# Order of the first slot's turn, group 5's gate, the first weight splits and the first biases in the head of a convolution with routed feed-forward

## Chip, cores, metric

One core of a Trainium2 chip runs the kernel. The time is device microseconds (us) of one execution, lower is better. Engines are named as in the profile: PE is TensorE (PEld its weight loads), DVE is VectorE, ACT is ScalarE, POOL is GpSimd, SP is SyncE, which here only issues DMAs. A letter q behind an engine's name is its instruction queue.

## What is computed

```python
# x (8, 3584, 192); weight (8 heads, 7 taps); modality_id (28672,); w_gate (192, 8); modality_bias (2, 8); w1 (8, 192, 1024); w2 (8, 1024, 192)
w = softmax(weight, axis=-1)                                  # 7 taps for each head of 24 channels
x = einsum('hk,bskhg->bshg', w, windows(x)).reshape(28672, 192)   # causal convolution along s
logits = x @ w_gate + modality_bias[modality_id]
e_idx, gate_w = argmax(logits), softmax(logits)[e_idx]
for e in range(8):                                            # one expert for each row
    mask = e_idx == e
    out[mask] = gate_w[mask, None] * (relu(x[mask] @ w1[e]) @ w2[e])
```

All is fp32. Products of fp32 data are taken in parts of TensorE's fast fp32 format: a value is split into a rounded part (a cast on ACT, "hi") and the rest (a subtraction on DVE, "lo").

## The kernel before

The rows of x come in 19 groups, of 1, 1, 2, 2, 2 and then 4 quads; a quad is 4 tiles of 112 rows. Groups 0 to 4 are chunk 0, groups 5 and 6 chunk 1, and so on. `body` takes a group through: eight convolutions, one for each head (`cv`, L282), copied from PSUM into the group's `y` buffers by ACT or DVE (L287, L289); the bias of its rows (`bias_of`, tile `bt`, two POOL instructions, L296 and L299); then for each quad a transposition on DVE (`turned`, L306), for groups from 5 on a split of it (`gx`, L98 cast on ACT and L99 subtraction on DVE), the product with the gate (`gt`, L326), its transposition (`lt`, L333) and the sum with the bias (`lg`, L336, L338); and the choice of an expert (`choose`, L349 to L366). `place` follows while the next group is convolved: counts by two products (`rp`, L376, L377), a scan (L382), positions (`pos`, L388, L389), their reduction (`row`, L391) and the row numbers (`idx`, L393). Then `send` scatters the group's rows from `y` to DRAM (`routed_rows`, L210, an indirect DMA on POOL for each tile). There are four `y` buffers: groups 0 to 4 hold y0, y1, y2, y3, y0, group 5 holds y1 and y2, group 6 y3 and y0. A buffer is free for the next group's convolutions when its scatters have landed.

A slot is up to 1024 rows of one expert. Its weights come by DMA (`raw1`, `raw2`) and are split (`w1b`, 4 parts, and `w2b`, 4 parts, by L98 and L99). Its rows come back from DRAM (`rows`, `ends`, `tags`, L661) after the last scatter of its chunk, are transposed on DVE (`turn`: `tp`, L688 and L689) and split into `sxh`, `sxl` and `sxs` (L696, L698). A step multiplies 128 hidden units (`hps`, five products, L712, two PSUM banks), applies relu on ACT (`hh`, L715), takes the rest on DVE (`hl`, L716), and two steps later multiplies by the second weights (`po`, L730, L734).

The head ends in `start(0)` (L903): all of chunk 0's groups, the first slot's loads, four splits of its first weights, then 26 steps (`AHEAD`) of the following groups' work, of which the gate's last instruction up to step 18 (`PIN`) is kept, and then the slot's `turn(0)`, to be placed behind that instruction. From there `run` emits steps of slots and pieces of groups side by side. A scheduler that simulates the engines places the emitted instructions in each engine's queue; each queue runs in order. In `run`, ACT keeps the order of emission. The convolutions of groups from 5 on, their gate products and their `rp` share two PSUM banks in turn (`bank`, tag t): group 5's gate halves take one each, group 6's head 0 and head 1 follow, then `rp`, then head 2 on head 1's bank, which so waits for head 1's copies.

Of the kernel before, what the change touches and what calls it, by code (L numbers as in the profile page):

```python
# [18 lines left out]
P = 128  # L19
# [7 lines left out]
WARM2 = 0  # L27
WAIT = 3
OUTS = 4
PIN = 18  # L30
AHEAD = 26
UNIT = 256
LONG = 512
# [10 lines left out]
def conv_then_routed_ffn(ctx, tc, x, weight, modality, w_gate, mod_bias, w1, w2, out):  # L44
# [89 lines left out]
    def make_bands():  # L134

        wide = P + MB
        line = raw1[0][0:1].rearrange("p c n -> p (c n)")[:, 0:H * wide].rearrange("p (h u) -> p h u", h=H)
        nc.vector.memset(line, 0.0)
        taps = const.tile([1, H, K], F32, name="taps")
        nc.sync.dma_start(out=taps, in_=weight.unsqueeze(0))  # L140
        peak = const.tile([1, H], F32, name="peak")
        nc.vector.tensor_reduce(out=peak, in_=taps, axis=AX.X, op=ALU.max)
        nc.vector.tensor_tensor(out=taps, in0=taps, in1=peak.unsqueeze(2).broadcast_to([1, H, K]), op=ALU.subtract)
        nc.scalar.activation(out=taps, in_=taps, func=AF.Exp)
        tot = const.tile([1, H], F32, name="tot")
        nc.vector.tensor_reduce(out=tot, in_=taps, axis=AX.X, op=ALU.add)
        nc.vector.tensor_scalar(out=tot, in0=tot, scalar1=1e-9, scalar2=None, op0=ALU.add)
        nc.vector.reciprocal(out=tot, in_=tot)

        first = MB - 1 + HALO - K + 1  # L150
        nc.vector.tensor_tensor(out=line[:, :, first:first + K], in0=taps,
                                in1=tot.unsqueeze(2).broadcast_to([1, H, K]), op=ALU.mult)
        lines = nc.dram_tensor("tap_lines", (H, wide), F32, kind="Internal").ap()
        nc.sync.dma_start(out=lines.unsqueeze(0), in_=line)
        band = xp.tile([P, H, MB], F32, name="band", tag="xr_0")
        nc.sync.dma_start(out=band, in_=bass.AP(lines.tensor, 0, [[1, P], [wide, H], [1, MB]]))
        hi = const.tile([P, H, MB], F32R, name="band_hi")
        lo = const.tile([P, H, MB], F32R, name="band_lo")
        split(hi, lo, band)
        return band, hi, lo  # L160

    def make_gate():


        wg = const.tile([P, NK, E], F32, name="wg")
        for q in range(P // Q):
            nc.scalar.dma_start(out=wg[q * Q:(q + 1) * Q], in_=w_gate.rearrange("(k c) e -> c k e", c=Q))
        wgs = const.tile([P, NK, 2 * E], F32R, name="wgs")
        nc.scalar.copy(out=wgs[:, :, 0:E], in_=wg)
        nc.vector.tensor_tensor(out=wgs[:, :, E:2 * E], in0=wg, in1=f(wgs[:, :, 0:E]), op=ALU.subtract)  # L170
        whole = const.tile([P, NK, P], F32, name="wg_whole", tag="w2b1")
# [58 lines left out]
    class Group:  # L230
# [60 lines left out]
        def bias_of(self):  # L291
            n = self.blocks
            self.lg = rt.tile([MB, NT, E], F32, name="lg")[:, 0:self.tiles]
            self.bt = rt.tile([MB, NT, E], F32, name="bt", bufs=1)[:, 0:self.tiles]
            m = mt[:, self.b0:self.b0 + self.nb, self.block:self.block + n].rearrange("p b s -> p s b")
            nc.gpsimd.tensor_tensor(  # L296
                out=self.bt.rearrange("p (s b) e -> p s b e", s=n), in0=m.unsqueeze(3).broadcast_to([MB, n, self.nb, E]),
                in1=step.unsqueeze(1).unsqueeze(1).broadcast_to([MB, n, self.nb, E]), op=ALU.mult)
            nc.gpsimd.tensor_tensor(out=self.bt, in0=self.bt,  # L299
                                    in1=start_row.unsqueeze(1).broadcast_to([MB, self.tiles, E]), op=ALU.add)  # L300
# [8 lines left out]
        def part_turned(self, q):  # L309
# [4 lines left out]
                both = xp.tile([P, 2, NK, NB, Q], F32R, name="gx", tag=self.place_x)  # L314
                self.gh, self.gl = both[:, 0, :, 0:self.nb], both[:, 1, :, 0:self.nb]
            at = slice(4 * q % NB, 4 * q % NB + 4)
            split(self.gh[:, :, at], self.gl[:, :, at], self.turned)
            return [(wg_parts, self.gh), (wg_parts, self.gl)]

        def gate(self, terms):  # L320
# [293 lines left out]
    class Slot:  # L614
# [59 lines left out]
        def split(self, part):  # L674

            i = self.i % 2
            if part < 4:
                c, ns = part % 2, slice(part // 2 * FF // 2, (part // 2 + 1) * FF // 2)
                split(w1b[i][:, c, ns], w1b[i][:, 2 + c, ns], raw1[i][:, c, ns])
            else:  # L680
                cs = slice((part - 4) * NF // 4, (part - 3) * NF // 4)
                split(w2b[i][:, cs, 0:D], w2b[i][:, cs, D:2 * D], raw2[i][:, cs, :])
# [220 lines left out]
    def start(i):  # L903
# [1 line left out]
            through("groups", 0)  # L905
            w2b.append(const.tile([P, NF, 2 * D], F32R, name="w2b1"))
        bring(lots.index((i, 0)))
        for part in range(4 if i == 0 else 8):
            made[i].split(part)
        for n in range(AHEAD if i == 0 else 0):  # L910
            advance()
            if n < PIN:
                pin = state["gate"]
        with tc.issue_after(pin) if i == 0 else nullcontext():
            warm(WARM2 if i == 0 else 0)
            made[i].turn(0)
# [35 lines left out]
```

## Time and profile before

| What | us |
|---|---|
| Three timed runs, median | 1293.76 (1290.85 to 1293.97) |
| Profiled execution | 1280.46, its span 1278.7 |
| PE busy | 1225.4 of the span |
| DVE busy | 975.8 |
| ACT busy | 692.6 |
| POOL busy | 543.5 |

The profiled execution is read as a time line that starts at 0. Behind the first 200 us PE has hardly a gap; the head, in which the first groups are convolved and scattered and the first slot is made ready, has most of PE's idle time. A row of the time line gives start, duration, engine, line, operation, output and input, count, and in brackets the idle time of that engine just before and what ended it.

### The profile page before, as it was taken

To read this page: it belongs to the slowest core of one execution; us is meant where nothing else is said; L and a number is where in the kernel's file an instruction comes from. 1 tells how busy PE (TensorE), PEld (TensorE's weight loads), DVE (VectorE), ACT (ScalarE), POOL (GpSimd) and SP (SyncE) were. 2 spreads that over 40 slices of the span, in tenths; PEclk is the share of its full clock that TensorE was granted. 3 is DMA by queue.
4 is the path that set the end of the run, shared out by engine and by line. 5 is a ranking of instruction groups with operands and counts; after the bars stand their busy time and mean duration, and the time that the engine had idled before them with its cause. 6 is when DMAs were issued, how large, how long until landed. Compare 5 with 4: busy or idle time off the path is not lost.

```text
span 1278.7 us, 23361 instructions
## 1 busy us (share of the span) xinstructions
PE 1225.4 (96%) x6986; PEld 1091.8 (85%) x6986; DVE 975.8 (76%) x2280; ACT 692.6 (54%) x1485; POOL 543.5 (43%) x574
## 2 busy tenths in 40 slices
PE   9568899999999999999999999999999999999996
PEld 7347778888898989898898889899898888888996
DVE  5668877787888778877888778877776666577895
ACT  2235565555555555555565656556545445446784
POOL 4736645344545343444545344353546221122222
PEclk9869999999999999999999999999999999999999
DMA  6578554426462445324363535344424244395341
GB/s 174 159 193 183 150 128 94 121 50 150 91 162 53 108 96 132 105 58 111 68 149 98 135 80 146 75 92 101 96 46 127 54 83 101 81 249 123 93 90 33
DMA packets 311420, 141.89 MB, mean 111 GB/s; under 512 B 225650, under 2 KB 297963, under 8 KB 311284
## 3 DMA queue, kind: packets, MB, share of 16 engines
q1 hardware_dynamic: 285668, 94.95, 35.5%
q0 software_dynamic: 23232, 44.30, 10.9%
q8 instruction: 57, 0.93, 0.3%
q10 hardware_dynamic: 2384, 1.06, 0.3%
q14 instruction: 79, 0.65, 0.2%
HBM read 118.16 MB, written 51.82 MB: 133 GB/s over the span
## 4 chain that ended last, share of the span: by engine, by line
PE 72%; DVE 9%; issue 7%; ACT 3%; POOL 2%; DMA 2%; DVEq 0%; SPq 0%; POOLq 0%; ACTq 0%
PE hps L712 34%; PE po L730 21%; PE po L734 10%; PE cv L282 5%; PE gt L326 3%; POOL out_dram L752 2%; DVE hl L716 1%; DVE gx L99 1%; DVE turned L306 1%; DVE w1b L99 1%; ACT hh L715 1%; DVE sxs L698 1%; DMA routed_rows<-y,idx 1%; DVE tp L688 1%; DMA xr<-in_x_dram 1%
## 5 line engine op out<-in xcount | busy, mean ns | idle before, releaser
L730 PE MATMUL po<-w2b,hh 128*128 128x384 f32 x1824 | 556.3, 359 | 0.9
L715 ACT ACTIVATE hh<-hps 128x512 fp32r<-128x512 f32 x456 | 272.7, 600 | 342.4 <-PE hps L712 329.7
L734 PE MATMUL po<-w2b,hl 128*128 128x192 f32 x1824 | 457.5, 252 | 0.0
L716 DVE SCALAR_TENSOR_TENSOR hl<-hps,hh 128x512 fp32r<-128x512 f32 x456 | 310.8, 685 | 172.6 <-ACT hh L715 169.7
L210 POOL DMA_INDIRECT routed_rows<-y,idx x256 | 269.0, 1051 | 338.0 <-DVE hl L716 118.1
L752 POOL DMA_INDIRECT out_dram<-o,tags x228 | 245.0, 1075 | 357.3 <-DVE o L748 188.8
L712 PE MATMUL hps<-sxh,w1b 128*128 128x512 f32 (+1 forms) x976 | 384.1, 397 | 6.6 <-DVE hl L716 6.5
L730 PEld LDWEIGHTS po<-w2b,hh 128*128 128x128 f32 x1824 | 343.3, 188 | 26.6 <-DVE o L748 4.5
L734 PEld LDWEIGHTS po<-w2b,hl 128*128 128x128 f32 x1824 | 346.9, 190 | 18.1
L712 PE MATMUL hps<-sxs,w1b 128*128 128x512 f32 (+1 forms) x976 | 290.3, 379 | 0.0
L712 PEld LDWEIGHTS hps<-sxh,w1b 128*128 128x128 f32 x976 | 184.4, 189 | 33.8 <-DVE hl L716 11.5
L712 PEld LDWEIGHTS hps<-sxs,w1b 128*128 128x128 f32 x976 | 179.1, 188 | 38.6 <-DVE sxs L698 0.4
L712 PE MATMUL hps<-sxl,w1b 128*128 128x512 f32 (+1 forms) x488 | 185.8, 381 | 0.0
L99 DVE TENSOR_TENSOR w1b<-raw,w1b 128x512 fp32r<-128x512 f32 x152 | 102.8, 686 | 17.5 <-ACT w1b L98 15.9
L287 ACT COPY y<-cv 112x192 f32<-112x192 f32 (+1 forms) x198 | 53.7, 318 | 100.4 <-PE cv L282 84.6
L746 ACT ACTIVATE lowp<-po,tags 128x192 f32<-128x192 f32 x228 | 84.2, 421 | 36.9 <-DVE o L748 32.4
L98 ACT CAST w1b<-raw 128x512 fp32r<-128x512 f32 x152 | 92.2, 619 | 7.9 <-DMA raw<-in_moe_w_dram 7.5
L712 PEld LDWEIGHTS hps<-sxl,w1b 128*128 128x128 f32 x488 | 93.1, 191 | 2.7
L99 DVE TENSOR_TENSOR w2b<-raw,w2b 128x384 fp32r<-128x384 f32 x152 | 82.0, 549 | 17.1 <-ACT w2b L98 17.1
L748 DVE SCALAR_TENSOR_TENSOR o<-po,tags,lowp 128x192 f32<-128x192 f32 x228 | 83.9, 409 | 13.8 <-ACT lowp L746 13.7
L98 ACT CAST w2b<-raw 128x384 fp32r<-128x384 f32 x152 | 75.8, 511 | 0.7
L306 DVE STREAM_TRANSPOSE turned<-y 128x768 f32<-128x768 f32 x64 | 60.8, 964 | 8.6 <-ACT y L287 8.2
(133 smaller groups left out, 973.2 us busy)
## 6 DMA issues: line engine op xcount, KB each, us to landing
raw<-in_moe_w_dram SPq DMA_DIRECT2D x38, 768.0 KB
raw<-in_moe_w_dram SPq DMA_DIRECT2D x38, 512.0 KB
raw<-in_moe_w_dram SPq DMA_DIRECT2D x76, 256.0 KB
xr<-in_x_dram SPq DMA_DIRECT2D x36, 384.0 KB
rows<-routed_rows SPq DMA_DIRECT2D x212, 64.0 KB
x<-in_x_dram SPq DMA_DIRECT2D x26, 384.0 KB
ends<-routed_rows SPq DMA_DIRECT2D x212, 32.0 KB
routed_rows<-filler SPq DMA_DIRECT2D x8, 776.0 KB
```

The costliest lines, as they stand in the source:

```text
L98: nc.scalar.copy(out=hi, in_=raw)
L99: return nc.vector.tensor_tensor(out=lo, in0=raw, in1=f(hi), op=ALU.subtract).ins
L210: state["scatter"] = nc.gpsimd.indirect_dma_start(out=scr, out_offset=bass.IndirectOffsetOnAxis(ap=idx, axis=0), in_=src, in_offset=None,).ins
L306: nc.vector.transpose(out=self.turned.rearrange("p k t c -> p t k c"), in_=self.ys[4 * q // NB][:, t0:t0 + 4, OVER:W].rearrange("p t (k c) ...
L712: nc.tensor.matmul(hps[:, u, :], wa[:, c, fs], mv[z], start=n == 0, stop=n == len(terms) - 1)
L715: nc.scalar.activation(out=hh, in_=hps, func=AF.Relu)
L716: state["result"] = nc.vector.scalar_tensor_tensor(out=hl, in0=hps, scalar=0.0, in1=f(hh), op0=ALU.max, op1=ALU.subtract).ins
L730: nc.tensor.matmul(po, hh[:, u, js], wb[:, c, :], start=c == 0, stop=c == NF - 1, skip_group_check=True)
L734: nc.tensor.matmul(po[:, 0:D], hl[:, u, js], wb[:, c, 0:D], start=False, stop=False, skip_group_check=True)
L746: nc.scalar.activation(out=lowp, in_=po[:, D:2 * D], func=AF.Copy, scale=gate)
L748: nc.vector.scalar_tensor_tensor(out=o, in0=po[:, 0:D], scalar=gate, in1=lowp, op0=ALU.mult, op1=ALU.add)
L752: st = nc.gpsimd.indirect_dma_start(out=out, out_offset=bass.IndirectOffsetOnAxis(ap=tag.bitcast(I32)[:, j, 1:2], axis=0), in_=o, in_offse ...
```

## The change

Five things change. `bias_of` makes the biases of groups 0 to 4 at once, in group 0 (`early_bias`, two POOL instructions of 112x256), and those of later groups behind the latest scatter that was emitted. In `start(0)` the first 23 steps of the following groups' work are emitted ahead of the four weight splits, and the splits and the slot's turn are placed behind the gate product that was emitted last. A cast of the first slot's weights waits for group 5's last `gx` subtraction. The last 3 of the 26 steps, group 5's choice among them, are placed behind the turn's last subtraction. And five small tiles of the setup (`taps`, `peak`, `tot`, `wg`, `wgs`) move into buffers of the second slot, which makes room.

```diff
-PIN = 18
+PIN = 23
+    FIRST_TILES = 4 * sum(QUADS_OF_GROUP[:WHOLE_Y])
-    def split(hi, lo, raw):
-        nc.scalar.copy(out=hi, in_=raw)
+    def split(hi, lo, raw, behind=None):
+        first = nc.scalar.copy(out=hi, in_=raw).ins
+        if behind is not None:
+            tc.add_manual_dep(first, behind.name, mybir.DependencyInfo(mybir.DependencyClass.Sync, mybir.DependencyReason.DATA),
+                              reason="later")
...
+    early_bias = const.tile([MB, FIRST_TILES // NB, NB, E], F32, name="early_bias")
...
+            if self.whole_y:
+                if self.block == self.b0 == 0:
+                    m, shape = mt[:, :, 0:early_bias.shape[1]].rearrange("p b s -> p s b"), list(early_bias.shape)
+                    nc.gpsimd.tensor_tensor(out=early_bias, in0=m.unsqueeze(3).broadcast_to(shape),
+                                            in1=step.unsqueeze(1).unsqueeze(1).broadcast_to(shape), op=ALU.mult)
+                    nc.gpsimd.tensor_tensor(out=early_bias, in0=early_bias,
+                                            in1=start_row.unsqueeze(1).unsqueeze(1).broadcast_to(shape), op=ALU.add)
+                self.bt = early_bias[:, self.block, self.b0:self.b0 + self.nb, :]
+                return
...
+            with tc.issue_after(state["scatter"]):
+                nc.gpsimd.tensor_tensor(
...
-            split(self.gh[:, :, at], self.gl[:, :, at], self.turned)
+            state["gx"] = split(self.gh[:, :, at], self.gl[:, :, at], self.turned)
...
-                split(w1b[i][:, c, ns], w1b[i][:, 2 + c, ns], raw1[i][:, c, ns])
+                split(w1b[i][:, c, ns], w1b[i][:, 2 + c, ns], raw1[i][:, c, ns],
+                      state["gx"] if self.i == 0 else None)
...
-        for part in range(4 if i == 0 else 8):
-            made[i].split(part)
-        for n in range(AHEAD if i == 0 else 0):
+        if i > 0:
+            for part in range(8):
+                made[i].split(part)
+            made[i].turn(0)
+            return
+        for n in range(PIN):
             advance()
-            if n < PIN:
-                pin = state["gate"]
-        with tc.issue_after(pin) if i == 0 else nullcontext():
-            warm(WARM2 if i == 0 else 0)
+        with tc.issue_after(state["gate"]):
+            for part in range(4):
+                made[i].split(part)
             made[i].turn(0)
+        for n in range(AHEAD - PIN):
+            with tc.issue_after(state["vector"]):
+                advance()
```

On POOL, from the scatters of group 2 (`y2`) to those of group 4 (`y0`), before:

```order
L210 DMA routed_rows<-y2_218,idx_558 238592x194 x8
L366 IOTA y3_219 112x8
L296 TENSOR_TENSOR bt_685<-mt_272,step_265 112x64
L299 TENSOR_TENSOR bt_685<-bt_685,both_263 112x64
L210 DMA routed_rows<-y3_219,idx_656 238592x194 x8
L366 IOTA y0_216 112x8
L296 TENSOR_TENSOR bt_888<-mt_272,step_265 112x128
L210 DMA routed_rows<-y0_216,idx_745 238592x194 x8
```

And after, to the bias of group 5 (`bt_863`):

```order
L217 DMA routed_rows<-y2_219,idx_547 238592x194 x8
L383 IOTA y3_220 112x8
L217 DMA routed_rows<-y3_220,idx_642 238592x194 x8
L383 IOTA y0_217 112x8
L217 DMA routed_rows<-y0_217,idx_728 238592x194 x8
L313 TENSOR_TENSOR bt_863<-mt_268,step_261 112x128
L383 IOTA y1_218 112x8
L383 IOTA y2_219 112x8
L316 TENSOR_TENSOR bt_863<-bt_863,both_259 112x128
```

Group 4's bias (`bt_685`) has left the queue, and both halves of group 5's stand behind group 4's eight scatters.

On DVE, from group 5's last turned quad, before (`tp_975` is the slot's turn, `lg_887` group 5's logits):

```order
L306 STREAM_TRANSPOSE turned_923<-y2_218 128x4x6x32
L99 TENSOR_TENSOR w1b0_89<-raw1_0_85,w1b0_89 128x512 x4
L99 TENSOR_TENSOR gx_916<-turned_901,gx_916 128x6x128
L333 STREAM_TRANSPOSE lt_919<-gt_903 128x256
L99 TENSOR_TENSOR gx_916<-turned_923,gx_916 128x6x128
L336 TENSOR_TENSOR lg_887<-lt_919,bt_888 112x64
L338 TENSOR_TENSOR lg_887<-lt_919,lg_887 112x64
L333 STREAM_TRANSPOSE lt_940<-gt_927 128x256
L336 TENSOR_TENSOR lg_887<-lt_940,bt_888 112x64
L338 TENSOR_TENSOR lg_887<-lt_940,lg_887 112x64
L349 TENSOR_REDUCE top_944<-lg_887 112x16
L688 STREAM_TRANSPOSE tp_975<-rows_838 128x512
```

And after (`lg_862` and `tp_927` are the same tiles; `cv_1007` is head 2 of group 6):

```order
L353 TENSOR_TENSOR lg_862<-lt_894,bt_863 112x64
L103 TENSOR_TENSOR gx_891<-turned_876,gx_891 128x6x128
L355 TENSOR_TENSOR lg_862<-lt_894,lg_862 112x64
L103 TENSOR_TENSOR gx_891<-turned_898,gx_891 128x6x128
L103 TENSOR_TENSOR w1b0_89<-raw1_0_85,w1b0_89 128x512 x2
L350 STREAM_TRANSPOSE lt_915<-gt_902 128x256
L103 TENSOR_TENSOR w1b0_89<-raw1_0_85,w1b0_89 128x512
L353 TENSOR_TENSOR lg_862<-lt_915,bt_863 112x64
L103 TENSOR_TENSOR w1b0_89<-raw1_0_85,w1b0_89 128x512
L355 TENSOR_TENSOR lg_862<-lt_915,lg_862 112x64
L296 COPY y3_220<-cv_1007 112x8x24
L706 STREAM_TRANSPOSE tp_927<-rows_821 128x512
```

The sum with the bias now stands ahead of both `gx` subtractions and of all four weight subtractions, and a copy of head 2 of group 6 ahead of the slot's turn. On PE the first slot's products change place too; before:

```order
L282 MATMUL cv_971<-x_755,band_237 112x384
L282 MATMUL cv_1024<-x_755,band_237 112x384
L712 MATMUL hps_989<-sxh_978,w1b0_89 128x512
L712 MATMUL hps_1076<-sxh_978,w1b0_89 128x512
L712 MATMUL hps_989<-sxl_979,w1b0_89 128x512
```

And after, where `cv_966`, `cv_1007` and `cv_1070` are heads 1, 2 and 4 of group 6:

```order
L289 MATMUL cv_966<-x_738,band_235 112x384
L289 MATMUL cv_1007<-x_738,band_235 112x384
L289 MATMUL cv_1070<-x_738,band_235 112x384
L730 MATMUL hps_972<-sxh_930,w1b0_89 128x512
L730 MATMUL hps_1059<-sxh_930,w1b0_89 128x512
```

Head 4, which takes head 2's bank, has moved ahead of the first step's products, and with it the wait for DVE's two copies of head 2. From the third `hl` on, DVE, ACT and PE have the same order in both programs.

## Rows read from the trace of the kernel before

**Rows 1.** The page's busy time of PE, with its share of the span and its instructions.

```profile
PE 1225.4 (96%) x6986; PEld 1091.8 (85%) x6986; DVE 975.8 (76%) x2280; ACT 692.6 (54%) x1485; POOL 543.5 (43%) x574
```

**Rows 2.** What PE waited for in the first 200 us: total us, times, longest us.

```profile
PE gt L326 <- ACT gx L98: 13.7, 4, 7.5
PE cv L282 <- DVE lt L333: 7.5, 3, 6.6
```

**Rows 3.** The time line of 34 to 52 us, PE, DVE and ACT: group 2's `idx`, then the wait for group 4's bias.

```profile
35.97 2.48 PE L326 MATMUL gt<-turned,wg_whole 128*128 128x128 f32 x20
...
38.60 0.19 DVE L336 TENSOR_TENSOR lg<-lt,bt 112x32 f32<-112x32 f32 x1 [0.92 <-POOL bt L299]
...
39.33 0.13 DVE L393 CAST idx<-row 112x8 int32<-112x8 f32 x1
...
50.79 0.19 DVE L336 TENSOR_TENSOR lg<-lt,bt 112x32 f32<-112x32 f32 x1 [6.68 <-POOL bt L299]
...
51.55 0.32 ACT L287 COPY y<-cv 112x192 f32<-112x192 f32 x1 [5.90 <-DMA routed_rows<-y,idx]
```

**Rows 4.** POOL's time line: scatters (L210) and biases.

```profile
33.07 0.94 POOL L210 DMA_INDIRECT routed_rows<-y,idx  x1 [0.28 <-POOL y L366]
...
40.24 0.97 POOL L210 DMA_INDIRECT routed_rows<-y,idx  x1 [1.68 <-ACT y L287]
...
48.99 0.94 POOL L210 DMA_INDIRECT routed_rows<-y,idx  x1 [0.30 <-issue]
...
50.44 0.32 POOL L299 TENSOR_TENSOR bt<-bt,both 112x64 f32<-112x64 f32 x1
52.37 1.01 POOL L210 DMA_INDIRECT routed_rows<-y,idx  x1 [1.61 <-ACT y L287]
...
62.82 0.97 POOL L210 DMA_INDIRECT routed_rows<-y,idx  x1 [0.17 <-POOL bt L296]
...
71.03 1.37 POOL L210 DMA_INDIRECT routed_rows<-y,idx  x1 [0.30 <-issue]
72.70 0.94 POOL L210 DMA_INDIRECT routed_rows<-y,idx  x1 [0.30 <-issue]
...
81.06 0.42 POOL L296 TENSOR_TENSOR bt<-mt,step 112x128 f32<-112x128 f32 x1 [6.52 <-DVE lg L336]
81.56 0.45 POOL L299 TENSOR_TENSOR bt<-bt,both 112x128 f32<-112x128 f32 x1
...
109.16 0.94 POOL L210 DMA_INDIRECT routed_rows<-y,idx  x1 [1.89 <-DVE hl L716]
```

**Rows 5.** The time line of 64 to 83 us, without POOL and SP: from the landing of the first weights to the slot's turn.

```profile
70.24 1.14 ACT L98 CAST w1b<-raw 128x512 fp32r<-128x512 f32 x2 [6.30 <-DMA raw<-in_moe_w_dram]
70.89 1.29 DVE L99 TENSOR_TENSOR w1b<-raw,w1b 128x512 fp32r<-128x512 f32 x2 [4.21 <-ACT w1b L98]
...
76.06 0.91 DVE L99 TENSOR_TENSOR gx<-turned,gx 128x768 fp32r<-128x768 f32 x1
...
77.03 3.12 PE L326 MATMUL gt<-gx,wg_parts 128*128 128x256 f32 x11
...
80.19 0.45 DVE L333 STREAM_TRANSPOSE lt<-gt 128x256 f32<-128x256 f32 x1 [2.83 <-PE gt L326]
...
81.40 0.70 DVE L688 STREAM_TRANSPOSE tp<-rows 128x512 f32<-128x512 f32 x1
...
82.36 0.54 ACT L287 COPY y<-cv 112x192 f32<-112x192 f32 x2 [3.90 <-PE cv L282]
...
82.95 1.62 PE L282 MATMUL cv<-x,band 128*112 128x384 f32 x2 [0.63 <-ACT y L287]
```

**Rows 6.** One piece of the chain that ended last, in order of time: the first step's products (start, us, what).

```profile
84.58 2.13 PE hps L712 x5
```

**Rows 7.** The time line of 84 to 98 us, DVE and ACT: group 5's place, the first two `hl` and the fourth.

```profile
87.33 0.36 DVE L289 COPY y<-cv 112x192 f32<-112x192 f32 x1
...
88.62 0.42 DVE L382 TENSOR_TENSOR_SCAN base<-keep,ad 112x128 f32<-112x128 f32 x1
...
89.65 0.60 ACT L715 ACTIVATE hh<-hps 128x512 fp32r<-128x512 f32 x1 [2.97 <-PE hps L712]
...
89.89 0.28 DVE L391 TENSOR_REDUCE row<-pos 112x16 f32<-112x128 f32 x1
...
90.29 0.69 DVE L716 SCALAR_TENSOR_TENSOR hl<-hps,hh 128x512 fp32r<-128x512 f32 x1
...
92.77 0.17 DVE L393 CAST idx<-row 112x16 int32<-112x16 f32 x1
...
93.00 0.69 DVE L716 SCALAR_TENSOR_TENSOR hl<-hps,hh 128x512 fp32r<-128x512 f32 x1
...
96.07 1.84 DVE L306 STREAM_TRANSPOSE turned<-y 128x768 f32<-128x768 f32 x2 [1.25 <-ACT y L287]
...
97.83 0.65 DVE L716 SCALAR_TENSOR_TENSOR hl<-hps,hh 128x512 fp32r<-128x512 f32 x1
```

**Rows 8.** Busy us of the engines (with instructions) by stretch: PE, PEld, DVE, ACT, POOL, then PE's granted clock, DMA share, GB/s.

```profile
68.00:72.00 4.00, 0.00 (x0) 0.00 (x0) 1.11 (x2) 1.14 (x2) 3.09 (x4) 0.50 0.85 207
...
80.00:84.00 4.00, 2.83 (x6) 1.17 (x5) 3.02 (x9) 1.27 (x4) 0.88 (x2) 0.50 0.65 129
84.00:88.00 4.00, 3.62 (x10) 2.26 (x10) 2.66 (x13) 0.81 (x2) 0.00 (x0) 0.50 1.09 338
88.00:92.00 4.00, 3.70 (x12) 2.23 (x13) 3.72 (x11) 2.32 (x6) 0.00 (x0) 0.91 1.06 307
...
100.00:110.00 10.00, 9.66 (x58) 8.60 (x58) 9.92 (x17) 7.75 (x15) 6.59 (x7) 1.00 0.60 105
```

More of the change, by code (lines that the diff above doesn't have):

```diff
@@ L138, in make_bands @@
         nc.vector.memset(line, 0.0)
-        taps = const.tile([1, H, K], F32, name="taps")
+        rest = raw1[1][0:1].rearrange("p c n -> p (c n)")
+        taps = rest[:, 0:H * K].rearrange("p (h k) -> p h k", h=H)
         nc.sync.dma_start(out=taps, in_=weight.unsqueeze(0))
-        peak = const.tile([1, H], F32, name="peak")
+        peak = rest[:, H * K:H * K + H]
         nc.vector.tensor_reduce(out=peak, in_=taps, axis=AX.X, op=ALU.max)
@@ L144, in make_bands @@
         nc.scalar.activation(out=taps, in_=taps, func=AF.Exp)
-        tot = const.tile([1, H], F32, name="tot")
+        tot = rest[:, H * K + H:H * K + 2 * H]
         nc.vector.tensor_reduce(out=tot, in_=taps, axis=AX.X, op=ALU.add)
@@ L162, in make_gate @@
     def make_gate():
-        wg = const.tile([P, NK, E], F32, name="wg")
+        early = raw1[1].rearrange("p c n -> p (c n)")[:, H * K + 2 * H:]
+        wg = early[:, 0:NK * E].rearrange("p (k e) -> p k e", e=E)
         for q in range(P // Q):
             nc.scalar.dma_start(out=wg[q * Q:(q + 1) * Q], in_=w_gate.rearrange("(k c) e -> c k e", c=Q))
-        wgs = const.tile([P, NK, 2 * E], F32R, name="wgs")
+        wgs = w1b[1].rearrange("p c n -> p (c n)")[:, 0:NK * 2 * E].rearrange("p (k e) -> p k e", k=NK)
         nc.scalar.copy(out=wgs[:, :, 0:E], in_=wg)
@@ L293, in bias_of @@
             self.lg = rt.tile([MB, NT, E], F32, name="lg")[:, 0:self.tiles]
+            if self.whole_y:
[7 more added lines that the diff above has]
+                return
             self.bt = rt.tile([MB, NT, E], F32, name="bt", bufs=1)[:, 0:self.tiles]
             m = mt[:, self.b0:self.b0 + self.nb, self.block:self.block + n].rearrange("p b s -> p s b")
[L296 to L300, printed above, removed]
+            with tc.issue_after(state["scatter"]):
+                nc.gpsimd.tensor_tensor(
+                    out=self.bt.rearrange("p (s b) e -> p s b e", s=n), in0=m.unsqueeze(3).broadcast_to([MB, n, self.nb, E]),
+                    in1=step.unsqueeze(1).unsqueeze(1).broadcast_to([MB, n, self.nb, E]), op=ALU.mult)
+                nc.gpsimd.tensor_tensor(out=self.bt, in0=self.bt,
+                                        in1=start_row.unsqueeze(1).broadcast_to([MB, self.tiles, E]), op=ALU.add)
         def turn(self, q):
```

## Prediction

> **What bounds the kernel now.** I read the page's busy times first: PE is busy for 96% of the span and DVE for 76% [rows 1], so an edit off PE pays only where PE waits. Then the list of PE's waits in the first 200 us: the gate waits 13.7 us for ACT's part of `gx` (7.5 at the longest), and the convolutions 7.5 us for DVE's `lt`, of which one wait is 6.6 [rows 2]. The reader is to see that the largest waits are group 5's, just those the change aims at. The time line shows what lies ahead of them: DVE waits 0.92 and then 6.68 us for POOL's biases, and ACT 5.90 us for scatters that have to land [rows 3]; POOL makes a bias between two groups' scatters and group 5's only after 6.52 us of waiting for DVE [rows 4]; DVE waits 4.21 us for the first weights' cast and then does the weights ahead of a `gx` [rows 5]. From there to 100 us the chain is convolutions, copies, first step, `hl` [rows 6, 7]. Last, the stretches: PE is at half clock with nothing to do at 68 to 72, still at half clock until about 88, and from 100 on DVE is busy 9.92 of 10 us [rows 8]. So what counts is when DVE's and ACT's common order after the first `hl`s begins: a shift of that is carried on, whatever its sign.
>
> **The biases at once.** Two larger POOL instructions early, while POOL has nothing else, cost nothing: group 0's scatters come much later than its bias is due. What goes is DVE's 0.92 for group 2 and 6.68 for group 4. The first does not all come back: the second gate product ends at 35.97 + 2.48 = 38.45, and its transposition and sum follow, so `idx` of 39.33 moves by about 0.4 only [rows 3]. The second ends 6.68 us earlier in DVE's time, but the next thing is y2's copy on ACT, which still waits for group 2's scatters; 51.55 becomes about 51.15. What is late next there is the landing.
>
> **POOL's queue.** Group 3's scatters stood behind group 4's bias (until 50.44 + 0.32), and waited 1.61 us more, to 52.37 [rows 4]. In the new order they follow group 2's last scatter (48.99 + 0.94 = 49.93, now 49.53) and one iota pair of 0.44: they begin at 49.97, 2.4 us earlier. Group 4's, before 62.82, lose the bias multiplication between as well: 2.7 earlier, and their end, 72.70 + 0.94 = 73.64, becomes 70.95. One of them took 1.37 at 71.03, beside a weight subtraction on DVE that began at 70.89 [rows 4, 5], where others take 0.94. That subtraction moves behind, so I take 0.43 off: 70.5. The loads of the slot's rows move with it; nobody waits for them.
> The Trainium skill, "SBUF — State Buffer", "Who interferes with whom", says that a subtraction with two SBUF inputs holds only the read side of the port pair that DVE and GpSimd share, while writing DMA descriptors needs the write side (it marks this as inferred). By that rule the scatter's 0.43 has another cause and stays, and the sum would be +1.9 in place of +1.5; the one row here speaks against it, weakly.
>
> **Group 5's bias** is now behind all eight scatters: 0.95 for the pair (81.06 to 82.01 before) and 0.25 for the iotas between give 70.5 + 1.2 = 71.7, against a bias that before was multiplied in POOL's gap at 62 and finished for the first sum in good time.
>
> **A wait added.** DVE is in order, and the sum `lg` of group 5's first half now stands ahead of both `gx` subtractions and all weight subtractions. So DVE waits from about 66.8 to 71.7 for POOL; queued behind are `gx`, hence PE's gate, and ACT's weight casts (they wait for the last `gx`). It takes the place of the wait of 4.21 for the weights [rows 5], which ended at 70.89. Then sum, `gx`, sum, `gx`: 2 x 0.2 + 2 x 0.91 = 2.2, done at 73.9 against 76.97. The gate takes 3.12: 77.0 against 80.15; `lt` 0.45: 77.5 against 80.64. **Gain so far 3.2.**
>
> **Where it goes.** PE's next are head 1 (1.62, to 79.1), ACT's two copies (0.54, to 79.7), head 2 (1.62, to 81.4) [rows 5]. But DVE's copy of head 2 (0.36 by the row of 87.33, [rows 7]) now stands ahead of the slot's `tp`. So `tp` begins at 81.75, where before it began at 81.40: the gain of 3.2 is given back, and 0.35 more. `tp` 0.70, the second copy 0.36: 82.8. On PE head 4 waits for that copy and stands ahead of the first step: 84.45. A product of the step at this clock takes 2.13 / 5 = 0.426 [rows 6]; the eight that the first `hh` needs give 3.4: 87.85. `hh` 0.60 begins at 87.9 against 89.65, and the first `hl` at 88.55 against 90.29: **1.75 earlier** [rows 7].
>
> **And given back again.** Group 5's choice now follows the turn. After the first `hl` (0.69, to 89.25) come mask and reciprocals, an estimate of 0.55, then the four `w2b` subtractions, which took 92.77 - 90.98 = 1.8 with what lies between, then copies 0.35: 91.95; the scan of 0.42 and `pos` (the scan to `row` took 89.89 - 88.62 = 1.27 plus 0.28 before) bring `pos` to 92.85 and `idx` to 93.5, which was 92.77. Head 3 of group 6 waits with its bank for `pos` (0.8 at full clock, half of 1.62): 93.65; two copies on ACT 0.54: 94.2; the second `hh` stands behind these on ACT, 0.60: the second `hl` at 94.85 against 93.00, **1.85 later**. Then copies 0.61 as a pair, a convolution 0.81, ACT's copies 0.54 and two turns of 1.84 lead to the fourth `hl` at 99.35 against 97.83: **+1.5** [rows 7]. From there the order on DVE, ACT and PE is the old one and DVE has no slack [rows 8], so the 1.5 stays to the end. Later groups' bias pairs, 0.95 each, now fall between a group's scatters; pace waits like 1.89 at 109.16 [rows 4] cover them, else 0 to 1.9 in all. The moved setup tiles are written again only for the second slot: 0, with nothing to uncover. **Sum +1.5** on the profiled execution's 1280.46, which lies 13.3 below the median of the three runs, so 1293.8 + 1.5 = 1295.3. A measurement of this kernel can tell about 0.3%, 3.9 us, from no change.
>
> **Rivals.** (1) *TensorE's clock comes back earlier.* PE now starts its busy stretch at 73.9 in place of 77.0 and has the gate, four convolutions and the step close together. The row of 80 to 84 shows 0.50 with PE busy 2.83 of 4, that of 88 to 92 0.91 [rows 8]: the clock rose after some 11 us of near steady work. If it rises by the middle of the gate, 1.55 of the gate, 4 x 0.8 less the parts under copies, and 8 x 0.2 of products come off: some 5.5. The sum is 1.5 - 5.5 = -4.0: 1289.8, or lower, to 1288.5. Against it: the convolutions still wait for copies, as before.
> The Trainium skill, "TensorE: Matmul & The Clock Gate", "What's actually happening", says that the low clock is the default and that activity releases it. By that rule the earlier start would bring the earlier rise of this rival; the rows agree as to direction.
> (2) *The half clock lasts longer*: the slower side. PE has holes at 79 to 80 and 81.4 to 82.8, waiting for copies, and again before head 3. If the clock is still 0.50 after 89, each stretch as long as the step's products (3.4 us at half clock) costs 1.7, and two such 3.2: 1.5 + 3.2 = +4.7, 1298.5. It decides from a rise later than 89. (3) *POOL becomes late*: the bias pairs between scatters are not covered, +0.95 to 1.9 more: 1297.0. (4) *The first `hl`'s gain is kept*: group 5's choice is absorbed by DVE's gaps, and the -1.75 is carried on: 1292.0. The change then does what it says.
>
> **Chances.** The sum as worked out with rivals 3 and 4 stays within 0.3%: 0.56. Rival 1, at its price, is just past 0.3%: 0.22. Rival 2: 0.22. The likeliest is the sum, 1295.3. The range takes in rival 1 down to 1288.5 and rival 2 to 1299.5, one repetition above its price.
>
> **What would show it.** Right: group 3's scatters begin near 50.0; DVE idle from about 67 to 71.7 for `bt`; the gate ends near 77.0; `tp` at 81.75; the first `hl` near 88.5, the second near 94.8, the fourth near 99.3; the clock at 1.00 from 88 or 89. Wrong: a clock of 1.00 before 84 (rival 1), 0.50 after 89 (rival 2), DVE's waits for `bt` or scatters after 100 us (rival 3), a second `hl` before 93.0 (rival 4). What overturns it most easily is that order after 89: if group 5's choice ends earlier than I add up, the sign turns.

## The result and the profile after

Over ten runs the changed kernel took 1299.68 us (median, 1291.13 to 1304.45), the kernel before on the same chip 1292.36 (10 runs, 1290.64 to 1293.97): a ratio of 1.0053, 95% interval [1.0038, 1.0068], some 6.9 us **slower** by that ratio. It was forecast within 0.3%, at +1.5 us. On another chip, where the kernel before takes 1280.09, a second set of runs gave 1.0033 [1.0020, 1.0047], 1285.64 us. The changed kernel's runs lie in two groups on each chip (two at 1291.13 and 1293.92, eight at 1298.66 to 1304.45; three at 1281.22 to 1282.78, five at 1285.29 to 1286.59), those of the kernel before show no such gap, and both profiles of the changed kernel are of the upper group, so part of the loss comes and goes from run to run. Chips differ by about 10 us here: the kernel before took 1278 to 1280 on three and 1290 to 1292 on the first and on one more. The profile of before that the prediction was read from has the time of the faster chips, the profile after that of the slower ones (1302.65, span 1300.9). What PE has to do is the same, to within 1% of [rows 1]:

```profile
PE 1234.8 (95%) x6986; PEld 1093.3 (84%) x6986; DVE 976.1 (75%) x2280; ACT 691.4 (53%) x1485; POOL 541.7 (42%) x566
```

The time line after, of the rows that answer to [rows 4, 5, 7] (group 3's first scatter, group 5's bias, its second gate product, the slot's turn, the first two `hl`):

```profile
53.81 0.94 POOL L217 DMA_INDIRECT routed_rows<-y,idx  x1 [0.28 <-issue]
...
74.16 0.46 POOL L316 TENSOR_TENSOR bt<-bt,both 112x128 f32<-112x128 f32 x1
...
87.73 2.72 PE L343 MATMUL gt<-gx,wg_parts 128*128 128x256 f32 x11 [0.58 <-DVE gx L103]
...
95.18 0.70 DVE L706 STREAM_TRANSPOSE tp<-rows 128x512 f32<-128x512 f32 x1
...
101.36 0.69 DVE L734 SCALAR_TENSOR_TENSOR hl<-hps,hh 128x512 fp32r<-128x512 f32 x1 [0.77 <-ACT hh L733]
...
107.58 0.69 DVE L734 SCALAR_TENSOR_TENSOR hl<-hps,hh 128x512 fp32r<-128x512 f32 x1 [1.27 <-ACT hh L733]
```

The first `hl` is 11 us later than the 90.29 of [rows 7], and the second follows by 6.2 in place of 2.7. A good part of the 11 lies in group 5's convolutions, in waits that [rows 2] and [rows 5] have nothing like. What was waited for from 55 to 80 us (total us, times, longest):

```profile
ACT y L294 <- remote: 20.1, 4, 10.0
...
DVE y L296 <- issue: 11.6, 1, 11.6
PE cv L289 <- remote: 5.4, 2, 2.8
```

"Remote" and "issue" mean that no event recorded on this core ends the wait; even some of DVE's small operations that follow one another stand 1.2 to 2 us apart there (72.65 to 77.57). I call these hold-ups. The clock in the stretches (columns as in [rows 8]) stays at half until almost 100 (0.51 in the row of 96 to 100), where before it rose between 88 and 92 (0.91):

```profile
88.00:92.00 4.00, 3.46 (x13) 2.61 (x13) 2.80 (x6) 1.89 (x4) 0.00 (x0) 0.50 0.49 54
...
96.00:100.00 4.00, 3.73 (x8) 2.65 (x9) 2.95 (x9) 1.65 (x4) 0.00 (x0) 0.51 1.10 334
100.00:110.00 10.00, 7.64 (x33) 5.02 (x33) 7.19 (x24) 4.74 (x13) 2.12 (x3) 1.00 0.82 154
```

### The profile page after: what moved, and what is told of

Its sections match the earlier page's. It is cut to its first block, busy times and chain, and to the rows that moved or that the text cites. A ratio compares the mean times of both kernels' runs of the same rounds, so it can differ in the third digit from the quotient of the medians.

```text
span 1300.9 us, 23351 instructions
## 1 busy us (share of the span) xinstructions
PE 1234.8 (95%) x6986; PEld 1093.3 (84%) x6986; DVE 976.1 (75%) x2280; ACT 691.4 (53%) x1485; POOL 541.7 (42%) x566
## 4 chain that ended last, share of the span: by engine, by line
PE 66%; issue 9%; DVE 8%; ACT 3%; POOL 2%; DMA 1%; DVEq 0%; SPq 0%; POOLq 0%; another core or an unknown queue 0%; ACTq 0%
PE hps L730 31%; PE po L748 20%; PE po L752 9%; PE cv L289 4%; PE gt L343 3%; POOL out_dram L770 2%; DVE hl L734 2%; DVE turned L323 1%; DVE sxs L716 1%; ACT hh L733 1%; DVE gx L103 1%; DVE tp L706 1%; ACT lowp L764 1%; DVE w1b L103 1%; DVE o L766 1%
## 5 line engine op out<-in xcount | busy, mean ns | idle before, releaser
L730 PE MATMUL hps<-sxs,w1b 128*128 128x512 f32 (+1 forms) x976 | 293.3, 382 | 0.0
L289 PE MATMUL cv<-x,band 128*112 128x384 f32 (+2 forms) x160 | 54.4, 464 | 28.4 <-DVE y L296 7.6
```

The lines of the kernel that those rows point to most:

```text
L289: nc.tensor.matmul(cv, wt[:, h, :], xt[:, :, hs], start=n == 0, stop=n == len(terms) - 1)
L730: nc.tensor.matmul(hps[:, u, :], wa[:, c, fs], mv[z], start=n == 0, stop=n == len(terms) - 1)
```

## The experiments

Kernels under one heading ran on one chip, beside the kernel before. Theory A, formed from this profile: the order behind 79 us makes the loss, by a wait for group 5's bias and by its choice behind the turn. Its rivals are the biases at once, and the hold-ups as a matter of chip or execution.

### Both kernels again, and the change in two parts (kernel before: 1280.09)

**r1_before** and **r2_after** are the two kernels unchanged. **e1_biases** is the kernel before with `early_bias` and the moved setup tiles alone, **e2_order** the changed kernel with the old `bias_of`:

```diff
# e1_biases, against the kernel before: early_bias, the setup tiles moved; later biases as before
+                self.bt = early_bias[:, self.block, self.b0:self.b0 + self.nb, :]
# e2_order, against the changed kernel
-                self.bt = early_bias[:, self.block, self.b0:self.b0 + self.nb, :]
...
-            with tc.issue_after(state["scatter"]):
```

Each line stands for its whole passage, which the section on the change shows.

> The kernel before, unchanged, profiled once more. Theory O (the order of the queues behind 79 us sets the result, the executions differ little): the head reads as before, group 5's convolutions run through within 52 to 61 us, the first hh starts within 1 us of 89.65, ratio 1.000 +- 0.002. Theory S (in the profiled execution of the changed kernel the engines were held up between 59 and 78 us, each hand-over from PE to ACT or DVE taking 2 to 3 us; that comes and goes from execution to execution and is no matter of the change): a second execution of the kernel before shows such hand-overs too, its first hh starts 5 to 12 us later than 89.65, and its span is near 1290, as the timed runs are, and not 1278.7.

> The changed kernel, unchanged, profiled once more. Theory O: the head as in the first profile of the changed kernel, the first hh at 100 to 101.5 us, clock 0.50 until about 99; ratio 1.005 +- 0.002. Theory S: the hold-ups between 59 and 78 us are of another size or gone; without them the first hh is at 87 to 90 us, as the prediction added up. The ratio is again 1.004 to 1.006.

> The kernel before with the biases of groups 0 to 4 made at once, and nothing of the new order (the five setup tiles moved, for room). POOL has group 3's scatters right behind group 2's. By the prediction's steps: DVE's 0.92 and 6.68 us waits go, scatters of groups 3 and 4 2.4 and 2.7 us earlier, the first weights still awaited: ratio 0.998 to 1.000. If the loss comes with the biases (scatters close behind one another hold up group 5's convolutions): ratio 1.003 to 1.006, the whole of the change.

> The changed kernel with the biases of all groups made one by one as in the kernel before: the new order of the slot's splits and turn alone. If the order makes the loss (DVE's sum with the bias, the copy ahead of the turn, the choice behind it): ratio 1.003 to 1.006. If the biases make it: 0.999 to 1.001. By the prediction's sum, which has the earlier scatters as a gain: 1.002 to 1.004.

Measured: r1 0.9997 [0.9988, 1.0006], r2 1.0033 [1.0020, 1.0047], e1 1.0003 [0.9994, 1.0011], e2 1.0041 [1.0028, 1.0054]. So e2, the order alone, has the loss; in e1 the biases at once change nothing that can be measured, though they do what they should (no wait for a bias in groups 2 and 4, group 3's scatters right behind group 2's). In e2 DVE waits 7.43 us for group 5's bias, since its second half stands behind group 4's scatters there too. The first `hh` of r1 is at 86.54, not within 1 us of 89.65 as theory O has it; that of r2 is at 89.08, as theory S has it, with a ratio below the 1.004 to 1.006 expected. No profile here has hold-ups, so r2's time line can be held against the prediction's steps one by one:

```profile
51.85 0.94 POOL L217 DMA_INDIRECT routed_rows<-y,idx  x1 [0.28 <-POOL y L383]
...
72.94 0.46 POOL L316 TENSOR_TENSOR bt<-bt,both 112x128 f32<-112x128 f32 x1
73.44 0.22 DVE L353 TENSOR_TENSOR lg<-lt,bt 112x64 f32<-112x64 f32 x1 [5.19 <-POOL bt L316]
...
75.59 2.71 PE L343 MATMUL gt<-gx,wg_parts 128*128 128x256 f32 x11 [5.45 <-DVE gx L103]
...
82.75 0.36 DVE L296 COPY y<-cv 112x192 f32<-112x192 f32 x1 [2.52 <-PE cv L289]
83.03 0.70 DVE L706 STREAM_TRANSPOSE tp<-rows 128x512 f32<-128x512 f32 x1
...
89.08 0.60 ACT L733 ACTIVATE hh<-hps 128x512 fp32r<-128x512 f32 x1 [1.29 <-PE hps L730]
89.71 0.69 DVE L734 SCALAR_TENSOR_TENSOR hl<-hps,hh 128x512 fp32r<-128x512 f32 x1 [1.26 <-ACT hh L733]
...
93.45 0.35 DVE L405 TENSOR_TENSOR pos<-rp,base 112x128 f32<-112x128 f32 x1
...
95.93 0.69 DVE L734 SCALAR_TENSOR_TENSOR hl<-hps,hh 128x512 fp32r<-128x512 f32 x1 [1.27 <-ACT hh L733]
...
100.61 0.65 DVE L734 SCALAR_TENSOR_TENSOR hl<-hps,hh 128x512 fp32r<-128x512 f32 x1
```

The wait for the bias, the copy ahead of the turn and the late second `hl` are there, each 1.1 to 1.7 us later than forecast (bias ready at 73.4 for 71.7, `tp` 83.03 for 81.75, the `hl`s at 89.71, 95.93 and 100.61 for 88.55, 94.85 and 99.35).

### The two terms of the order, one by one (kernel before: 1290.21)

```diff
# e3_bias_early: later groups' biases where the scheduler puts them
-            with tc.issue_after(state["scatter"]):
# e4_choice_before: the last 3 steps not behind the turn
-            with tc.issue_after(state["vector"]):
# e5_both: both lines out
# e6_weights_free: the first casts don't wait for group 5's last gx
-                      state["gx"] if self.i == 0 else None)
+                      None)
```

> The changed kernel, but group 5's bias (and later groups') is not placed behind the latest scatter: both its halves stand ahead of group 4's scatters. DVE, ACT and PE have the order of the changed kernel. Theory A (two terms: the wait for the bias behind the scatters holds gx and the gate until 73.4, and the choice behind the turn delays the second hh by 3): DVE no longer idles 5.2 us for the bias, the gx subtractions start near 68 in place of 73.6, the first hh comes 2 to 4 us earlier than 89.08, but the second hh still follows the first by 6.2 and the fourth by 10.1; ratio 1.000 to 1.002. Theory B (the wait for the bias is covered by that for the slot's rows, which follow the scatters anyway): first hh unchanged within 1 us, ratio 1.003 to 1.005.

> The changed kernel, but group 5's choice is not placed behind the slot's turn; the wait for the bias stays. Theory A: the second hh follows the first by 2.7 to 3.5 us as in the kernel before, in place of 6.2, and the fourth by 7.3 in place of 10.1; first hh at 89 to 91; ratio 1.001 to 1.003. Theory C (only the first hh counts, what is behind it is absorbed by DVE's later gaps): ratio 1.003 to 1.005.

> Both at once: group 5's bias early, and the choice not behind the turn. What is left of the change is the biases at once, the gate ahead of the weight splits, and the tiles. Theory A: the two terms add up, first hh at 85 to 87, fourth 7.3 behind it, ratio 0.998 to 1.000. If something else of the new order costs (the copy of head 2 ahead of the turn, head 4 ahead of the first step): 1.002 or more.

> The changed kernel without the wait of the first weight casts for group 5's last gx subtraction; the scheduler then puts the first cast on ACT ahead of one gx cast, a weight subtraction on DVE ahead of a gx, and the slot's turn ahead of the copies. Theory A: the bias's wait stays, so the first hh stays within 1.5 us of 89.08, the second follows by 6; ratio 1.003 to 1.005. If the splits behind the gate make the loss: 1.000 to 1.002.

Measured: 1.0079 [1.0062, 1.0095], 1.0072 [1.0058, 1.0086], 1.0065 [1.0045, 1.0085], 1.0063 [1.0047, 1.0080]. All four are slower alike, e5 too: theory A is not borne out here, and none of the ratios expected for e3, e4 and e6 came. Every one of these profiles has the hold-ups, and a first `hh` at 100 to 103. So the ratios say nothing of the two terms, but the later rows still do: where the choice stands behind the turn (e3, e6), the fourth `hh` follows the first by 10.1, and where it doesn't (e4, e5), by 7.1.

### The kernel before a third time, and e5's kernel again (kernel before: 1280.18)

> The kernel before, unchanged, a third profile. So far its two profiles come from executions near 1280, and all runs of the batch of the four variants from near 1290 and above, where PE, ACT and DVE show hold-ups in group 5's convolutions (57 to 76 us) that no profile near 1280 shows. If the kernel before runs near 1290 here, theory H (the hold-ups belong to the chip and hit the kernel before too): its convolutions of group 5 are stretched as well, first hh at 92 to 98. If only the biases made at once bring the hold-ups: first hh near 88, no such waits. If it runs near 1280: first hh at 86 to 90 and no hold-ups.

> The kernel of e5 (group 5's bias early, the choice not behind the turn) once more. If the kernel before runs near 1280 here: theory A (two terms of the order make the loss) has the first hh at 85 to 87 and a ratio of 0.998 to 1.001; if the loss stays at 1.003 or more, theory A falls. If it runs near 1290: ratio 1.005 to 1.008 as in e5, and the loss is in the hold-ups, which the order of the slot's turn does not touch.

Measured: r3_before 0.9990 [0.9980, 1.0000], e7 0.9993 [0.9981, 1.0004], without hold-ups in either. With both lines out the loss is gone, as theory A has it. r3's time line shows what the kernel before does when its head starts earlier and the weights land early:

```profile
58.78 0.83 ACT L98 CAST gx<-turned 128x768 fp32r<-128x768 f32 x1 [0.87 <-DVE srow L570]
...
64.96 1.14 ACT L98 CAST w1b<-raw 128x512 fp32r<-128x512 f32 x2 [4.24 <-DMA raw<-in_moe_w_dram]
...
71.53 3.12 PE L326 MATMUL gt<-gx,wg_parts 128*128 128x256 f32 x11
...
78.15 0.71 DVE L688 STREAM_TRANSPOSE tp<-rows 128x512 f32<-128x512 f32 x1 [2.18 <-DMA rows<-routed_rows]
...
84.78 0.60 ACT L715 ACTIVATE hh<-hps 128x512 fp32r<-128x512 f32 x1 [2.00 <-PE hps L712]
```

In [rows 5] the first cast of the weights was at 70.24 and the second gate product at 77.03. Here they are 5.3 and 5.5 us earlier, and the turn waits for the slot's rows instead. Of that, 3.1 us are there already at group 5's first `gx` cast, which in the profile of [rows 5] was

```profile
61.88 0.83 ACT L98 CAST gx<-turned 128x768 fp32r<-128x768 f32 x1 [0.87 <-DVE srow L570]
```

### The biases and the early bias on a fourth chip (kernel before: 1278.37)

> The kernel of e1 (the biases at once alone) once more; on a chip where the kernel before runs near 1280 it gave 1.0003. If the kernel before runs near 1290 here: if the biases at once bring the hold-ups in group 5's convolutions, ratio 1.004 to 1.008 and hold-ups between 55 and 76 us in the profile; if the hold-ups belong to the chip and hit every kernel alike, ratio 0.999 to 1.001, with hold-ups; if only the new order brings them, ratio 0.999 to 1.001 and none. If it runs near 1280: 0.999 to 1.001 again.

> The kernel of e3 (the changed kernel with group 5's bias early, the choice still behind the turn) once more. If the kernel before runs near 1280 here: theory A says the first hh comes at 86 to 88, without a wait for the bias, the second 6.2 behind it and the fourth 10.1 behind it, some 3 later than in the kernel before; ratio 1.001 to 1.003, between e7's 0.9993 and r2's 1.0033. If the wait for the bias alone makes the loss: 0.999 to 1.000. If it runs near 1290: as e3, 1.006 to 1.009.

Measured: e8 1.0012 [1.0001, 1.0022], e9 1.0022 [1.0012, 1.0031]; the kernel before ran near 1280, so the question of the hold-ups stayed unanswered. e9's ratio is as expected, its first `hh` earlier than the 86 to 88. It waits for no bias, and its turn and `hh` are

```profile
78.52 0.70 DVE L706 STREAM_TRANSPOSE tp<-rows 128x512 f32<-128x512 f32 x1
...
84.65 0.60 ACT L733 ACTIVATE hh<-hps 128x512 fp32r<-128x512 f32 x1 [1.37 <-PE hps L730]
...
90.85 0.61 ACT L733 ACTIVATE hh<-hps 128x512 fp32r<-128x512 f32 x1
...
94.75 0.60 ACT L733 ACTIVATE hh<-hps 128x512 fp32r<-128x512 f32 x1 [0.15 <-PE hps L730]
```

against e7's, whose choice is not behind the turn,

```profile
79.33 0.70 DVE L706 STREAM_TRANSPOSE tp<-rows 128x512 f32<-128x512 f32 x1
...
87.13 0.60 ACT L733 ACTIVATE hh<-hps 128x512 fp32r<-128x512 f32 x1 [2.66 <-PE hps L730]
...
89.84 0.61 ACT L733 ACTIVATE hh<-hps 128x512 fp32r<-128x512 f32 x1
...
94.24 0.60 ACT L733 ACTIVATE hh<-hps 128x512 fp32r<-128x512 f32 x1 [0.62 <-PE hps L730]
```

So 1.0033 (r2) falls to 1.0022 with the bias early, by about 0.11%, and to 0.9993 with the choice moved as well, by a further 0.29%, if ratios on different chips of the faster kind may be set against one another. The intervals of r2 and e9 overlap, so the share of the bias is not clear of noise; that of the choice is. But 0.29% is 3.7 us, and the profiles show less. With the choice behind the turn the first `hh` comes sooner behind the turn's `tp`, 6.1 us in place of 7.8, and the second later, 12.3 in place of 10.5; the fourth follows `tp` by 16.2 in place of 14.9. So the choice costs 1.3 us up to there (1.5 in e3 against e5, 1.0 in the first profile after against e4). The medians of e9 and e7 are 2.0 us apart; the rest of the 0.29% is that the kernel before was 1.8 us faster on e9's chip. For the bias the profiles show 1.7 us: from group 5's first `gx` cast to `tp` r2 takes 21.0 us, e9 and e7 19.3. The whole wait of 5.19 is not won, because in e9 DVE then waits 4.77 for the weights' cast, which on ACT stands behind a copy that waits 4.29 for scatters to land.

## Where the time is, by stretches

Worked out from the starts of group 5's first `gx` cast, of the turn's `tp` and of `hh` in the profiles on the faster chips (us; the first three columns are starts, the others distances, the last to the end of the span):

| kernel | `gx` | `tp` | 1st `hh` | to 4th | to 12th | to 29th | to the end |
|---|---|---|---|---|---|---|---|
| before, r1, r3 | 61.9, 59.5, 58.8 | 81.4, 79.1, 78.2 | 89.7, 86.5, 84.8 | 7.2, 7.3, 7.2 | 26.8, 28.2, 28.7 | 59.2, 59.2, 63.3 | 1095.9, 1095.9, 1095.4 |
| e1, e8 (biases) | 62.6, 62.5 | 79.8, 79.5 | 85.8, 85.4 | 7.2, 7.2 | 28.9, 28.8 | 61.2, 59.0 | 1097.9, 1098.0 |
| e2 (order) | 61.5 | 84.8 | 90.4 | 10.1 | 26.4 | 58.9 | 1098.6 |
| r2 (changed kernel) | 62.0 | 83.0 | 89.1 | 10.1 | 26.3 | 60.2 | 1098.6 |
| e9 (bias early) | 59.2 | 78.5 | 84.7 | 10.1 | 26.2 | 61.2 | 1097.8 |
| e7 (both lines out) | 60.1 | 79.3 | 87.1 | 7.1 | 26.2 | 60.1 | 1098.4 |

r2 against the mean of the three profiles of before: +2.0 at group 5's first cast, +1.5 from there to `tp`, -1.4 to the first `hh`, +2.9 to the fourth, -1.6 to the twelfth, -0.3 to the 29th, and +2.8 in all the rest: 5.9, as 1284.3 - 1278.4.

The last column falls into two groups without overlap: 1095.4 to 1095.9, and 1097.8 to 1098.6 for every kernel with a piece of the change, e1 and e2 alike. These two share only the moved setup tiles, and from the third `hl` on DVE and ACT run the same instructions in the same order in r1, r2, e1 and e2. The grouped lines of 300 to 1150 us (busy us, mean ns of one) show `hps` products longer by 2 to 3 ns; r1_before,

```profile
L712 PE MATMUL hps<-sxs,w1b 128*128 128x512 f32 x670 | 208.7, 393 | 0.0
...
L712 PE MATMUL hps<-sxl,w1b 128*128 128x512 f32 x335 | 132.1, 394 | 0.0
```

and e1_biases:

```profile
L726 PE MATMUL hps<-sxs,w1b 128*128 128x512 f32 x668 | 210.3, 396 | 0.0
...
L726 PE MATMUL hps<-sxl,w1b 128*128 128x512 f32 x334 | 132.2, 396 | 0.0
```

For the `sxs` products the mean is 396 in all eleven profiles with moved tiles, on either kind of chip, and 393 in the three without. From start to start on PE, the pairs that begin with an `hps` product take 3.6 to 3.8 us more in these 850 us than in the kernel before, those of `po` products with one another 1.9 to 2.1 less, and all together 1.3 to 2.0 more (r2, e1, e2, e7, e8, e9). Over the 1096 us of the last column that would be, by an estimate from these numbers, 1.7 to 2.6, most of what the column shows. That points to the tiles' move as the cause, with the products as the place where it shows; the move by itself was not run, and why the products would take longer was not found. e7 has the late end too (1098.4) and makes it up ahead of it, so its total is that of before.

## Why the prediction came out as it did

**The give-back was right in place and size.** The second `hl` was forecast 1.85 later after a first 1.75 earlier, a swing of 3.6. Measured: the second `hh` follows by 6.2 in place of 2.7, a swing of 3.5, in e2, r2, e9 and all kernels with the choice behind the turn, and 2.7 without (e7). What stands behind the turn was added up well as a whole: the fourth `hl` follows `tp` by 17.6 in r2 (100.61 - 83.03), as forecast (99.35 - 81.75). The net price of the choice is smaller than the swing, 1.3 us in e9 against e7, since the first `hh` gains by it.

**The step that failed: "the first `hl` at 88.55 against 90.29: 1.75 earlier", and in it the turn, "`tp` begins at 81.75, where before it began at 81.40".** Two things in it were mis-sized. First, the 81.40 and the 90.29 were read from one execution. In the two other profiles of before the first `hh` comes 3.1 and 4.9 us earlier, at 86.5 and 84.8; of that, 2.4 and 3.1 us are there already at group 5's first `gx` cast. DVE's wait for the weights' first cast, 4.21 in [rows 5], is 1.64 and 2.04 there, so the wait that the change takes away is mostly not there; and the turn waits for the slot's rows, of which the prediction says that nobody waits for them. r1_before, and behind it r2_after:

```profile
75.11 1.95 SPq L661 DMA_DIRECT2D rows<-routed_rows  x4
...
79.14 0.71 DVE L688 STREAM_TRANSPOSE tp<-rows 128x512 f32<-128x512 f32 x1 [2.83 <-DMA rows<-routed_rows]
```

```profile
74.08 1.95 SPq L678 DMA_DIRECT2D rows<-routed_rows  x4
...
83.03 0.70 DVE L706 STREAM_TRANSPOSE tp<-rows 128x512 f32<-128x512 f32 x1
```

In r1 and r3 the turn begins 4.0 and 4.1 us behind the issue of these loads, as soon as they have landed. In r2 it begins 9.0 behind it, since the wait that the change adds, 5.19 for the bias behind POOL's last scatter, and then the copy of head 2 ahead of `tp` (82.75) hold it; in e9, without the wait for the bias, still 6.7 behind it. So in r2 the loads are issued 1.0 us earlier than in r1, and the turn begins 3.9 later. Against the mean of three executions the first `hh` is 2.1 later, not 1.75 earlier. Second, "group 3's scatters begin at 49.97" came at 51.85 in r2, so the bias was ready 1.7 later than forecast; in e9 and e7 they begin at 49.64 and 50.08, as forecast.

**"The biases at once cost nothing" failed, in the setup.** The time line of r1_before, and behind it that of r2_after:

```profile
14.90 0.20 DVE L177 COPY wg_whole<-wg 32x48 f32<-32x48 f32 x1
...
16.45 1.09 DVE L99 TENSOR_TENSOR band_lo<-band,band_hi 128x896 fp32r<-128x896 f32 x1
16.47 2.91 PE L282 MATMUL cv<-x,band 128*112 128x96 f32 x24 [1.19 <-DVE y L289]
```

```profile
14.87 0.90 POOL L304 TENSOR_TENSOR early_bias<-mt,step 112x256 f32<-112x256 f32 x1 [5.13 <-DVE mt L202]
15.28 0.53 DVE L183 COPY wg_whole<-raw 32x48 f32<-32x48 f32 x1
...
15.85 0.72 POOL L306 TENSOR_TENSOR early_bias<-early_bias,both 112x256 f32<-112x256 f32 x1
15.94 0.68 DVE L183 COPY wg_whole<-raw 32x48 f32<-32x48 f32 x1
...
17.68 1.09 DVE L103 TENSOR_TENSOR band_lo<-band,band_hi 128x896 fp32r<-128x896 f32 x1
17.70 4.80 PE L289 MATMUL cv<-x,band 128*112 128x96 f32 x24 [2.61 <-DVE y L296]
```

Two copies that take 0.18 to 0.20 took 0.53 and 0.68 beside the longer bias instructions, 0.83 more in all, and PE waited 2.61 in place of 1.19. It is not the moved tile that they read: in e2, with the tiles moved and the old biases, the four copies take 0.18 to 0.20. In r2 PE then also ran group 0's convolutions at half clock, 4.80 for 2.91: the granted clock is 0.54 at 17 to 19 us and 0.50 at 19 to 23, where r1 has 1.00. The wait alone does not decide this, since e9, with a wait of 2.83, has 1.00 and 2.88. Of the ten profiles with the biases at once, five have 0.50 at 21 to 23, and their first scatter leaves at 29.5 to 30.2, e1's and e8's among them; in the other five it leaves at 27.3 to 27.7, and in the four with the old biases at 25.8 to 28.5. So in r2 the first scatter left at 29.71, against 25.8 to 27.8 in the three profiles of before, and ate the 2.4 us that the earlier bias had won for group 3's.

The Trainium skill, "SBUF — State Buffer", "Who interferes with whom", has a DVE copy in a two-port mode and a GpSimd instruction exclude one another for the whole of an instruction. The trace agrees in so far as each of the two copies ends 0.04 to 0.05 us behind the POOL instruction beside it (15.81 and 15.77, 16.62 and 16.57); which mode the copies run in it does not show.

The remark of the Trainium skill, "SBUF — State Buffer", "Who interferes with whom", marked there as inferred, by which a DVE subtraction of two SBUF inputs leaves descriptor writing alone, and which the prediction weighed, is not borne out. In r2 a scatter took 1.64 beside the `gx` subtractions, where others take 0.94:

```profile
63.11 1.88 DVE L103 TENSOR_TENSOR gx<-turned,gx 128x768 fp32r<-128x768 f32 x2
...
63.23 1.64 POOL L217 DMA_INDIRECT routed_rows<-y,idx  x1 [0.30 <-issue]
```

Over the whole of r2, the 64 scatters that begin while a subtraction of `gx`, `w1b` or `w2b` is running on DVE take 1.32 on average, the other 192 take 0.96.

**"Moved setup tiles: 0" failed**, as far as the last column of the table can be put down to them: 2 to 3 us, spread over a thousand, about half of r2's loss, and in no place that the prediction looked at.

**"The 1.5 stays to the end" holds only in part.** With the order of before, kernels that are early at the fourth `hh` lose some of it by the twelfth (28.2 to 28.9 in r1, r3, e1 and e8, with the fourth at 92.0 to 93.8, against 26.8 in the first profile, with the fourth at 96.9): in r1_before ACT waits 3.42 us ahead of 120.89 for a store of results (`out_dram`) to land, and r3, e1 and e8 wait 3.1 to 3.8 in the same place. With the new order the distance is 26.2 to 26.4, whether the fourth comes at 94.2 (e7) or at 100.5 (e2). So r2, 5.0 behind the mean of before at the fourth `hh`, is 3.4 behind it at the twelfth, because the kernel before loses time there in two of its three profiles.

**The rivals.** The clock (rivals 1 and 2) did not decide it on the faster chips: it rose in r2's stretch 88 to 92 (0.90) as before (0.91 in [rows 8]). In the first profile after it did stay at 0.50 until almost 100, as rival 2 said, but behind the hold-ups and not by the holes at 79 to 83. Rival 3 found no wait in r2; rival 4 does not hold, since the second `hh` stands 6.2 behind the first in every run with the choice behind the turn. The measured time lies in the case slower by over 0.3%, which had 0.22, but not for that case's reason. Two sums among the rivals are off by 0.2: two stretches of 1.7 are 3.4, not 3.2, and 1.5 + 1.9 on 1293.8 is 1297.2, not 1297.0. As an absolute time it is 0.2 above the range's upper end; as a difference to the kernel before, +6.9 by the ratio on one chip and +4.2 on another (+5.6 by the medians there), where the range went to +5.7. That the difference came no further from +1.5 is luck in part: r2's turn is 3.5 later than in the mean of the three profiles of before, not 0.35, the end loses 2.8 of which the prediction has nothing, and 1.9 come back between the fourth and the 29th `hh`, of which it has nothing either.

**What stays open.** On two chips that are 10 us slower with the kernel before, group 5's convolutions are held up by what the profile cannot name, and every kernel with the gate ahead of the splits loses 0.5 to 0.8%, e5 too, which loses nothing elsewhere. No profile of the kernel before was taken on such a chip, nor were the biases alone timed there, so it was not settled whether the hold-ups hit the kernel before as well or come with the change. The 10 us that it loses there itself are about the 11.6 by which the first `hh` is later in the first profile after than in r2, which would fit hold-ups in both; it is not shown. Nor is it known what sets the clock of group 0's convolutions.

## What to carry to other kernels

A wait whose end is a DMA's landing varies from execution to execution: before building a change on it, read it in several profiles, since here it was 4.2 us in one and 1.6 to 2.0 in two. When work is pulled ahead in an in-order queue, price what is pushed behind it: with the choice behind the turn the first step came 1.7 us sooner behind it and the second 1.8 later. Setup work is not free because its engine is idle: look at the other engine's instructions beside it, and at where moved tiles end up.

## What was not expected of the hardware

Small fp32 copies on DVE took 0.53 and 0.68 us in place of 0.18 to 0.20 beside a 112x256 instruction on POOL, and ended just behind it. Scatters on POOL that begin while a subtraction of `gx`, `w1b` or `w2b` runs on DVE took 1.32 us on average in place of 0.96 (r2). `hps` products over the same shapes took 396 ns in place of 393 with tiles moved in SBUF, over a thousand microseconds and in every profile with the move. And the kernel before took 1278 to 1280 us on three chips and 1290 to 1292 on two others, where profiles of the changed kernels show waits of up to 11.6 us that no recorded event ends.
